# Attention and SwiGLU on one core: two queues for the first load of k, longer first dummies, and one bias moved

## The chip, the cores and the metric

The kernel runs on one core of a Trainium2 chip. A core has five engines with instruction streams of their own: TensorE (PE: matmuls and transposes into PSUM; its weight loads, PEld, overlap them), VectorE (DVE), ScalarE (ACT), GpSimd (POOL) and SyncE (SP). SP, ACT and POOL also issue DMAs. The metric is the device time of one execution in microseconds. The kernel before takes 332.2 us, the median of 4 runs (332.03 to 332.84).

## What is computed

Causal attention with a sliding window of 64, over 8 batches, 8 heads, 576 positions and 64 per head, followed by a SwiGLU feed-forward block over the 4608 tokens:

```python
scores = scale * np.matmul(q, k.transpose(0, 1, 3, 2))
mask = (rel >= 0) & (rel < window)          # window = 64
scores = np.where(mask, scores, -1000000000.0)
attn = np.exp(scores - max) ; attn = attn / sum
x = (attn @ v), heads side by side          # 4608 x 512
g = x @ w_gate ; silu = g * (1.0 / (1.0 + np.exp(-g)))
out = (silu * (x @ w_val)) @ w_out          # 512 -> 1536 -> 512
```

All inputs and the output are float32; the kernel computes its matmuls in bfloat16.

## The kernel before

The 4608 tokens are cut into 36 chunks of 128 for attention and 9 chunks of 512 for the feed-forward block. For a chunk n of attention, q and k are loaded with positions on partitions, transposed by TensorE (later by DMA), and copied from PSUM to `qT` and `kT`; 24 small matmuls give the scores (`S`, line 421), ScalarE takes the exponential into `pt` (line 431), matmuls with v give the sums (`A`, two phases, line 471), VectorE divides (`norm`, lines 490 and 493) into `xb`, and TensorE transposes the result (`X`, line 568) to `xT`. The feed-forward step `F` (line 602) takes 128 of the 1536 columns: four gate matmuls, four value matmuls, a tanh on ScalarE (608), and, in step `U`, two operations on VectorE (611, 613) into `hT`. `O` multiplies by `w_out`.

The order at the start is written out by hand. `LOADS` is the order in which loads are issued; `STEPS` the order of everything else. Each token makes instructions and appends them to the queue of their engine, and each engine runs its own queue strictly in that order, waiting on semaphores for what others make. The tokens that matter here:

- `f:0` (line 285): the first 128 positions of k, in two halves of four heads, into the float32 tile `ff`; both DMAs are issued by SP (line 290). It is the first token of `LOADS`, so it stands before everything else on its queue.
- `init`: clears and constants on VectorE: the zeros `wz` for dummies, the identity, the mask, and the bias mask `nmask` (line 268), then clears in `kT` and `va` (270, 272); and one exponential of ScalarE (line 256) that brings its table load forward.
- `q:0`, `kq:n`, `v:n`, `w:a:b`: loads issued by POOL, which convert to bfloat16. Their order: q0, q1, k1, q2, k2, v1, v0, q3, k3, v2, v3, then weights 7 to 8, 1, 5, chunks 4 and 5, weights 3, 4, 6, and so on.
- `ca:0:0`, `cd:0:1`: the casts of `ff` to the bfloat16 tile `cc`, half of the head pairs on ScalarE, half on VectorE (lines 299, 301). Each waits for both halves of `f:0`.
- `T:0:1`, `T:0:0`: the transposes of `cc`, two each (line 309); `ea:0:1` and `ed:0:0` copy them into `kT`.
- `TQ:n`, `TK:n`: four transposes of q or k of chunk n (309); `qa`, `qd`, `ka`, `kd`: the copy to `qT` or `kT` on ACT or DVE. `xa`, `xd`: the same for `X`.
- `warm:45:64` (line 339): 45 dummy matmuls of zeros, 64 columns each (line 345); nobody reads their result.
- `W:1` (`fill`, line 350): one dummy matmul of zeros with 512 columns (line 357).
- `B:n` (`bias`, line 396): two matmuls of 512 columns that put the mask of chunk n into the two PSUM banks of its scores ahead of them (line 401). Chunks 0, 1 and 3 have such a bias; for the others `M:n` multiplies the exponentials by the mask on VectorE (line 437).
- `ld:n`: loads of a later chunk.

The queue of TensorE follows the tokens; a dependency is only what data and buffers ask for. `fill` takes the bank that has been free longest and doesn't reserve it.

Of the kernel before, what the change touches and what calls it, by code (L numbers as in the profile page):

```python
# [7 lines left out]
B, H, S, D = 8, 8, 576, 64  # L8
DM, DFF = H * D, 1536
T = B * S  # L10
# [139 lines left out]
class _Kernel:  # L150
# [13 lines left out]
    v:4 w:9:10 w:0:1 kq:6 v:7 kq:7 w:10:12  # L164
    """
    STEPS = """
    warm:45:64 B:0 B:1 ca:0:0 cd:0:1 T:0:1 T:0:0 ea:0:1 TQ:0 ld:8 wo:0:6 ed:0:0 qa:0 W:1 TQ:1 S:0 qd:1 TK:1
    ld:9 kd:1 W:1 TQ:2 S:1 qd:2 TK:2 kd:2 W:2 S:2 W:1 A0:0 A0:1 A1:0 A1:1 ld:10 N:0 TQ:3 B:3 qa:3 N:1 TK:3 X:0
    ka:3 xa:0 M:2 W:1 S:3 X:1 A0:2 xd:1 A1:2 ld:11 N:2 W:1 A0:3 A1:3 N:3 W:1 X:2 F:0:7:0:256 xd:2 U X:3
    F:0:8:0:384 xd:3 F:0:1 U U F:0:5 U TK:4 TQ:4 ld:12 ka:4 TQ:5 F:0:7:256:512 qd:4 TK:5 qa:5 F:0:8:384:512 U  # L170
    S:4 U F:0:3 kd:5 M:4 S:5 U F:0:4 M:5 U F:0:6 U F:0:2 U A0:4 A0:5 A1:4 ld:13 wo:6:12 A1:5 F:0:9 N:4 N:5 X:4
    F:0:0 U xa:4 X:5 U TK:6 xa:5 TQ:6 ld:14 F:1:0:0:128 ka:6 U F:1:1:0:256 qa:6 TQ:7 U F:1:2:0:256 qd:7 S:6
    TK:7 U F:1:3:0:256 kd:7 F:0:10 M:6 U U A0:6 S:7 A1:6 ld:15 TQ:8 TK:8 N:6 F:0:11 M:7 ka:8 qd:8 X:6 A0:7
    xa:6 S:8 U A1:7 ld:16 F:1:4:0:384 N:7 F:1:5:0:384 U X:7 U TQ:9 xa:7 F:1:6:0:384 M:8 qa:9 TK:9 U F:1:7 kd:9
    TD:10 U A0:8 S:9 A1:8 ld:17 F:1:8 N:8 M:9 X:8 TQ:11 xa:8 F:1:9 U qd:11 A0:9 TK:11 U A1:9 ka:11 F:1:10 N:9
    TK:12 U X:9 ka:12 TQ:12 F:1:11 xd:9 qd:12 TD:13 S:10 U S:12 F:1:0:128:512 M:10 F:1:1:256:512 M:12 A0:10 U
    S:11 A1:10 U F:1:2:256:512 F:1:3:256:512 N:10 F:1:4:384:512 U XD:10 F:1:5:384:512 O:0:0 U U U M:11 O:0:1
    A0:11 S:13 A1:11 O:0:2 N:11 M:13 X:11 O:0:3 xd:11 F:1:6:384:512 U TD:14 TD:15
    """

    def __init__(self, nc, q, k, v, wg, wv, wo, out):
# [103 lines left out]
    def first_load(self, n):  # L285
        (_, b, s, L), = self.segs(128 * n, 128)
        for u in range(2):
            d = self.ff[n][64 * u:64 * u + 64].rearrange("p h j d -> p h (j d)")
            a = self.k[b, 4 * u:4 * u + 4, s:s + L, :].rearrange("h (p j) d -> p h (j d)", j=2)
            self.g.op("sp", lambda e, d=d, a=a: e.dma_start(d, a), writes=[("ff", n, u)], dma=True)  # L290

    def cast(self, n, half, eng):
        hs = slice(2 * half, 2 * half + 2)
# [489 lines left out]
```

The softmax here doesn't subtract the row's maximum and nothing guards it: scores larger than these inputs give would overflow.

## Time and profile before

| | |
|---|---|
| median of the 4 runs | 332.2 us (332.03, 332.04, 332.35, 332.84) |
| profiled execution, its own time | 331.92 us |
| span of its instructions | 329.8 us |
| busy TensorE, VectorE, ScalarE, GpSimd | 324.6, 217.2, 136.0, 116.5 us |
| gate and value matmuls (L602) | 2 x 468, 112.5 us each |
| output matmuls (L635) | 420, 97.8 us |
| first load of k, from issue to landing | 2.7 us (first half), 3.6 us (second) |
| first gate matmuls (chunk 0, column block 7) | start at 17.76 us |

The times of a view are microseconds from the start of the span. A busy row cuts the span into 40 slices of 8.2 us, each digit the busy share in tenths. In the timeline a line gives start, length, engine, line of the kernel, operation, what is written and read, how often, and in brackets the idle time before it with what ended it. In the chain of waits, which is followed back from the last instruction, each piece has its start and length; adjacent pieces of one kind are merged. A matmul's record contains the time to drain, so the distance between two starts tells the speed, not the length of one.

The first rows of the two queues that the change touches, from the timeline:

```profile
0.74 1.41 SPq L290 DMA_DIRECT2D ff<-in_k_dram  x2
0.74 1.28 ACT L256 ACT_TABLE_LOAD   x1 [0.74 <-PEq L768]
...
2.04 0.20 ACT L256 ACTIVATE wup<-wup 128x1 f32<-128x1 f32 x1
...
5.17 0.42 ACT L299 ACTIVATE cc<-ff 128x256 bf16<-128x256 f32 x1 [2.93 <-DMA ff<-in_k_dram]
```

SP issues the two halves one after the other; ScalarE loads its table, makes the dummy exponential, and then has nothing to do until the halves have landed.

### The profile page before, as it was taken

Reading aid. Unit: us, or ns where it says so; the run is one execution under the profiler, and the core shown is the slowest. Engines: PE = TensorE matmul, PEld = TensorE weight load, DVE = VectorE, ACT = ScalarE, POOL = GpSimd, SP = SyncE. Lnnn points to the kernel's source line nnn. Section 1 sums busy time; section 2 is a strip of 40 time slices with the busy share of each in tenths; the row PEclk is TensorE's granted clock in tenths of the full one; section 3 lists DMA queues with packets and bytes.
Section 4 is the critical chain, followed back from the end, with each engine's and each line's share of the span. In section 5 each row is a group of like instructions: output and inputs, shape, how many; then the busy total and the mean of one; then the engine's idle time right before and its main releaser. Section 6 shows DMA issues by size and latency. Waiting matters only on the chain.

```text
span 329.8 us, 8380 instructions
## 1 busy us (share of the span) xinstructions
PE 324.6 (98%) x3543; PEld 166.6 (51%) x3543; DVE 217.2 (66%) x457; ACT 136.0 (41%) x247; POOL 116.5 (35%) x145
## 2 busy tenths in 40 slices
PE   7999999999999999999999999999999999999996
PEld 5565665564455454544445454545454544444444
DVE  5589999993467858485857676767676766555520
ACT  3735566453344344343425252525243432332222
POOL 8999999957017506060706060100000000000000
PEclk9999999999999999999999999999999999999999
DMA  9999999999999999999999999442424111100012
GB/s 107 165 168 172 158 182 155 160 141 179 193 172 148 171 160 104 153 89 169 90 169 81 175 71 188 67 111 44 118 35 128 34 64 34 64 34 32 32 63 99
DMA packets 169365, 38.56 MB, mean 117 GB/s; under 512 B 160368, under 2 KB 164848, under 8 KB 169328
## 3 DMA queue, kind: packets, MB, share of 16 engines
q0 software_dynamic: 123600, 18.75, 85.7%
q1 hardware_dynamic: 45584, 19.21, 28.8%
q8 instruction: 28, 0.46, 0.6%
q10 hardware_dynamic: 144, 0.07, 0.1%
q14 instruction: 9, 0.07, 0.1%
HBM read 37.75 MB, written 9.44 MB: 143 GB/s over the span
## 4 chain that ended last, share of the span: by engine, by line
PE 97%; DVE 2%; issue 0%
PE ps L602 57%; PE ps L635 28%; PE ps L421 3%; PE ps L534 2%; PE ps L309 2%; PE ps L471 2%; PE ps L665 1%; PE ps L568 1%; PE ps L401 1%; PE ps L357 1%; DVE xb L493 1%; DVE mask L267 0%; DVE hT L613 0%; DVE pt L437 0%; DVE rc L490 0%
## 5 line engine op out<-in xcount | busy, mean ns | idle before, releaser
L611 DVE SCALAR_TENSOR_TENSOR uu<-sig,ps 128x512 bf16<-128x512 bf16 (+3 forms) x117 | 75.3, 643 | 66.0 <-ACT sig L608 65.7
L602 PE MATMUL ps<-xT,Wg 128*128 128x512 bf16 (+3 forms) x468 | 112.5, 363 | 0.1
L602 PE MATMUL ps<-xT,Wv 128*128 128x512 bf16 (+3 forms) x468 | 112.5, 363 | 0.0
L608 ACT ACTIVATE sig<-ps 128x512 bf16<-128x512 f32 (+3 forms) x117 | 66.0, 565 | 88.9 <-PE ps L602 88.8
L635 PE MATMUL ps<-Wo,hT 128*128 128x512 bf16 x420 | 97.8, 379 | 0.0
L613 DVE SCALAR_TENSOR_TENSOR hT<-uu,ps 128x512 bf16<-128x512 bf16 (+3 forms) x117 | 75.5, 645 | 4.0
L371 POOL DMA_DIRECT2D va<-in_v_dram x40 | 40.3, 1041 | 88.3 <-PE ps L534 86.6
L602 PEld LDWEIGHTS ps<-xT,Wv 128*128 128x128 bf16 x468 | 45.0, 98 | 48.8 <-DVE hT L613 0.5
L602 PEld LDWEIGHTS ps<-xT,Wg 128*128 128x128 bf16 x468 | 43.9, 98 | 45.9 <-DVE hT L613 0.2
L635 PEld LDWEIGHTS ps<-Wo,hT 128*128 128x128 bf16 x420 | 39.9, 98 | 46.6
L431 ACT ACTIVATE pt<-ps 128x512 bf16<-128x512 f32 x72 | 37.8, 600 | 27.0 <-PE ps L421 26.9
L647 ACT ACTIVATE ost<-ps 128x512 f32<-128x512 f32 x35 | 20.9, 597 | 66.0 <-PE ps L635 65.9
L283 POOL DMA_DIRECT2D qn<-in_q_dram x40 | 41.3, 1052 | 2.8 <-issue 2.0
L283 POOL DMA_DIRECT2D kn<-in_k_dram x39 | 40.6, 1062 | 1.0 <-DMA kn<-in_k_dram 1.0
L437 DVE TENSOR_TENSOR pt<-pt,mask 128x512 bf16<-128x512 bf16 x66 | 24.3, 418 | 0.2
L556 DVE TENSOR_TENSOR xb<-ps,rp 128x448 bf16<-128x448 f32 (+1 forms) x36 | 18.5, 514 | 1.2
L553 DVE RECIPROCAL rp<-ps 128x7 f32<-128x7 f32 (+1 forms) x36 | 6.7, 187 | 15.4 <-PE ps L534 15.4
L421 PE MATMUL ps<-qT,kT 64*64 64x64 bf16 (+1 forms) x864 | 16.0, 205 | 0.1
L421 PEld LDWEIGHTS ps<-qT,kT 64*64 64x64 bf16 x864 | 12.4, 109 | 7.0 <-DVE hT L613 4.2
L534 PE MATMUL ps<-va,pt 64*64 64x65 bf16 x728 | 11.5, 193 | 0.1
L493 DVE TENSOR_TENSOR xb<-ps,rc 128x256 bf16<-128x256 f32 x24 | 10.2, 424 | 0.8
L534 PEld LDWEIGHTS ps<-va,pt 64*64 64x64 bf16 x728 | 9.3, 108 | 0.6 <-DVE hT L613 0.4
(50 smaller groups left out, 106.3 us busy)
## 6 DMA issues: line engine op xcount, KB each, us to landing
out_dram<-ost SPq DMA_DIRECT2D x35, 256.0 KB, 2.8
qn<-in_q_dram POOLq DMA_DIRECT2D x32, 128.0 KB, 6.5
va<-in_v_dram POOLq DMA_DIRECT2D x32, 128.0 KB, 6.4
kn<-in_k_dram POOLq DMA_DIRECT2D x31, 128.0 KB, 7.5
Wo<-in_moe_w_out_dram POOLq DMA_DIRECT2D x2, 768.0 KB, 12.0
Wg<-in_moe_w_gate_dram POOLq DMA_DIRECT2D x8, 128.0 KB, 5.1
Wv<-in_moe_w_val_dram POOLq DMA_DIRECT2D x8, 128.0 KB, 5.1
Wg<-in_moe_w_gate_dram POOLq DMA_DIRECT2D x2, 256.0 KB, 5.4
```

The source lines that it names most:

```text
L283: self.g.op("pool", lambda e, d=d, a=a: e.dma_start(d, a), writes=ks, dma=True)
L371: g.op("pool", lambda e, d=d, a=a: e.dma_start(d, a), writes=ks, dma=True)
L421: r = e.matmul(sv[h][o:o + 64, c, q0:q1], self.kT[ps, c, kk:kk + 64], qT[ps, c, q0:q1], start=not biased, stop=not biased or c == 3 and kk ...
L431: g.op("act", lambda e, po=po, si=si: e.activation(po, si, ACTF.Exp, scale=SCALE), reads=[bk], writes=[pk])
L437: "dve", lambda e: e.tensor_tensor(po, po, m, ALU.mult), reads=[pk, "mask"], writes=[pk]))
L534: r = e.matmul(bb[b][0][ws, 65 * sl:65 * sl + 65], self.pt[(n + j) % self.NP][ks, h, ws], vv[ks, h, 0:65], start=m == q[0], stop=m == q[-1])
L602: r = e.matmul(bank[:, 0:n], W[:, kk, f * 128:f * 128 + 128], xT[:, kk, t0:t1], start=(kk == 0), stop=(kk == NK - 1))
L608: g.op("act", lambda e: e.activation(sig[:, 0:n], G[:, 0:n], ACTF.Tanh, scale=0.5), reads=[gk], writes=[("sig", i)])
L611: g.op("dve", lambda e: e.scalar_tensor_tensor(uu[:, 0:n], sig[:, 0:n], 1.0, G[:, 0:n], ALU.add, ALU.mult), reads=[("sig", i), gk], writes ...
L613: g.op("dve", lambda e: e.scalar_tensor_tensor(hT[:, f, t0:t1], uu[:, 0:n], 0.5, V[:, 0:n], ALU.mult, ALU.mult), reads=[("uu", i), vk], wr ...
L635: r = e.matmul(OB[:, :], hT[:, f, 128 * u:128 * u + 128], self.Wo[:, f, :], start=(f == 0), stop=(f == NF - 1))
L647: g.op("act", lambda e: e.activation(ost[:, :], OB[:, :], ACTF.Copy), reads=[ok], writes=[("ost", io)])
```

## The change

The second half of `f:0` is issued by ScalarE and not by SP. The 45 first dummies get 96 columns in place of 64. `B:1` goes from behind `B:0` to behind `TQ:0`. Of the eight dummies of 512 columns four go: one of the pair before `S:2`, the one behind `S:2`, the one behind `N:2` and the one before `X:2`; and the one behind `qa:0` goes to before `TQ:0`. The order of the loads stays; of the rest of `STEPS` only the line breaks differ.

```diff
-    warm:45:64 B:0 B:1 ca:0:0 cd:0:1 T:0:1 T:0:0 ea:0:1 TQ:0 ld:8 wo:0:6 ed:0:0 qa:0 W:1 TQ:1 S:0 qd:1 TK:1
-    ld:9 kd:1 W:1 TQ:2 S:1 qd:2 TK:2 kd:2 W:2 S:2 W:1 A0:0 A0:1 A1:0 A1:1 ld:10 N:0 TQ:3 B:3 qa:3 N:1 TK:3 X:0
-    ka:3 xa:0 M:2 W:1 S:3 X:1 A0:2 xd:1 A1:2 ld:11 N:2 W:1 A0:3 A1:3 N:3 W:1 X:2 F:0:7:0:256 xd:2 U X:3
...
+    warm:45:96 B:0 ca:0:0 cd:0:1 T:0:1 T:0:0 ea:0:1 W:1 TQ:0 B:1 ld:8 wo:0:6 ed:0:0 qa:0 TQ:1 S:0 qd:1 TK:1
+    ld:9 kd:1 W:1 TQ:2 S:1 qd:2 TK:2 kd:2 W:1 S:2 A0:0 A0:1 A1:0 A1:1 ld:10 N:0 TQ:3 B:3 qa:3 N:1 TK:3 X:0
+    ka:3 xa:0 M:2 W:1 S:3 X:1 A0:2 xd:1 A1:2 ld:11 N:2 A0:3 A1:3 N:3 X:2 F:0:7:0:256 xd:2 U X:3 F:0:8:0:384
...
-            self.g.op("sp", lambda e, d=d, a=a: e.dma_start(d, a), writes=[("ff", n, u)], dma=True)
+            self.g.op(("sp", "act")[u], lambda e, d=d, a=a: e.dma_start(d, a), writes=[("ff", n, u)], dma=True)
```

More of the change, by code (lines that the diff above doesn't have):

```diff
@@ L166 @@
     STEPS = """
-    warm:45:64 B:0 B:1 ca:0:0 cd:0:1 T:0:1 T:0:0 ea:0:1 TQ:0 ld:8 wo:0:6 ed:0:0 qa:0 W:1 TQ:1 S:0 qd:1 TK:1
-    ld:9 kd:1 W:1 TQ:2 S:1 qd:2 TK:2 kd:2 W:2 S:2 W:1 A0:0 A0:1 A1:0 A1:1 ld:10 N:0 TQ:3 B:3 qa:3 N:1 TK:3 X:0
-    ka:3 xa:0 M:2 W:1 S:3 X:1 A0:2 xd:1 A1:2 ld:11 N:2 W:1 A0:3 A1:3 N:3 W:1 X:2 F:0:7:0:256 xd:2 U X:3
-    F:0:8:0:384 xd:3 F:0:1 U U F:0:5 U TK:4 TQ:4 ld:12 ka:4 TQ:5 F:0:7:256:512 qd:4 TK:5 qa:5 F:0:8:384:512 U
-    S:4 U F:0:3 kd:5 M:4 S:5 U F:0:4 M:5 U F:0:6 U F:0:2 U A0:4 A0:5 A1:4 ld:13 wo:6:12 A1:5 F:0:9 N:4 N:5 X:4
@@ L172 @@
[L172 to L176, printed above, removed]
@@ L177 @@
-    S:11 A1:10 U F:1:2:256:512 F:1:3:256:512 N:10 F:1:4:384:512 U XD:10 F:1:5:384:512 O:0:0 U U U M:11 O:0:1
-    A0:11 S:13 A1:11 O:0:2 N:11 M:13 X:11 O:0:3 xd:11 F:1:6:384:512 U TD:14 TD:15
+    warm:45:96 B:0 ca:0:0 cd:0:1 T:0:1 T:0:0 ea:0:1 W:1 TQ:0 B:1 ld:8 wo:0:6 ed:0:0 qa:0 TQ:1 S:0 qd:1 TK:1
+    ld:9 kd:1 W:1 TQ:2 S:1 qd:2 TK:2 kd:2 W:1 S:2 A0:0 A0:1 A1:0 A1:1 ld:10 N:0 TQ:3 B:3 qa:3 N:1 TK:3 X:0
+    ka:3 xa:0 M:2 W:1 S:3 X:1 A0:2 xd:1 A1:2 ld:11 N:2 A0:3 A1:3 N:3 X:2 F:0:7:0:256 xd:2 U X:3 F:0:8:0:384
@@ new lines @@
+    xd:3 F:0:1 U U F:0:5 U TK:4 TQ:4 ld:12 ka:4 TQ:5 F:0:7:256:512 qd:4 TK:5 qa:5 F:0:8:384:512 U S:4 U F:0:3
+    kd:5 M:4 S:5 U F:0:4 M:5 U F:0:6 U F:0:2 U A0:4 A0:5 A1:4 ld:13 wo:6:12 A1:5 F:0:9 N:4 N:5 X:4 F:0:0 U
+    xa:4 X:5 U TK:6 xa:5 TQ:6 ld:14 F:1:0:0:128 ka:6 U F:1:1:0:256 qa:6 TQ:7 U F:1:2:0:256 qd:7 S:6 TK:7 U
+    F:1:3:0:256 kd:7 F:0:10 M:6 U U A0:6 S:7 A1:6 ld:15 TQ:8 TK:8 N:6 F:0:11 M:7 ka:8 qd:8 X:6 A0:7 xa:6 S:8 U
+    A1:7 ld:16 F:1:4:0:384 N:7 F:1:5:0:384 U X:7 U TQ:9 xa:7 F:1:6:0:384 M:8 qa:9 TK:9 U F:1:7 kd:9 TD:10 U
@@ L179 @@
+    A0:8 S:9 A1:8 ld:17 F:1:8 N:8 M:9 X:8 TQ:11 xa:8 F:1:9 U qd:11 A0:9 TK:11 U A1:9 ka:11 F:1:10 N:9 TK:12 U
+    X:9 ka:12 TQ:12 F:1:11 xd:9 qd:12 TD:13 S:10 U S:12 F:1:0:128:512 M:10 F:1:1:256:512 M:12 A0:10 U S:11
+    A1:10 U F:1:2:256:512 F:1:3:256:512 N:10 F:1:4:384:512 U XD:10 F:1:5:384:512 O:0:0 U U U M:11 O:0:1 A0:11
+    S:13 A1:11 O:0:2 N:11 M:13 X:11 O:0:3 xd:11 F:1:6:384:512 U TD:14 TD:15
     """
```

## The prediction

> **What bounds the kernel now.** I read the busy slices first, then the shares of the chain that ended last, then the first 20 us of that chain in order of time, and last the times from issue to landing of the early loads.
>
> ```profile
> PE   7999999999999999999999999999999999999996
> ...
> POOL 8999999957017506060706060100000000000000
> ...
> PE 97%; DVE 2%; issue 0%
> ```
>
> TensorE is busy throughout (its row is below 9 only in the first and the last slice of 8.2 us) and holds 97% of the chain, while POOL issues loads without rest for the first 70 us. So a microsecond is won or lost in the start, where TensorE still waits for others, and it stays won only if no later load is waited for. Here is the start in the chain's order (start, length, what):
>
> ```profile
> 4.33 1.89 PE ps L401 x4
> 6.21 0.85 PE ps L309 x8
> 7.07 0.43 PE ps L357
> ...
> 10.58 0.44 DVE kT L301
> ...
> 11.50 0.32 PE ps L357
> 11.83 0.65 PE ps L471 x38
> 12.72 0.42 DVE xb L493
> ...
> 14.79 0.68 DVE pt L437 x2
> ...
> 16.23 0.32 PE ps L357
> ...
> 17.20 0.32 PE ps L357
> 17.53 0.40 PE ps L568 x4
> 17.92 0.87 PE ps L602 x8
> ...
> 19.02 4.86 PE ps L602 x24
> ```
>
> Biases, transposes and scores run to 11.8, attention and VectorE's normalizing to 18.9, and from 19.0 gate and value matmuls stand back to back. Dummies (L357) are links of this chain at 7.07, 11.50, 16.23 and 17.20. Rows of the timeline show the speed, and the cast that waits for the first load of k:
>
> ```profile
> 1.02 2.58 PE L345 MATMUL ps<-wz 128*128 128x64 bf16 x45 [1.02 <-DVE wz L255]
> ...
> 4.33 1.89 PE L401 MATMUL ps<-nmask,ident 128*128 128x512 bf16 x4 [0.72 <-DVE nmask L268]
> ...
> 5.17 0.72 DVE L301 CAST cc<-ff 128x256 bf16<-128x256 f32 x1 [0.59 <-DMA ff<-in_k_dram]
> ...
> 12.79 0.59 PE L401 MATMUL ps<-nmask,ident 128*128 128x512 bf16 x2
> ```
>
> The same bias matmul comes every 0.42 us at 4.33 ((1.89-0.63)/3) and every 0.21 at 12.79: the clock doubles between. The transposes at 9.25 are the first with a faster member, so it doubles at about 9.6; the windows' clock column reads 1.00 all along and does not show it. TensorE stood still for 0.72 us before 4.33, and ran with hardly a gap from 4.33 to the doubling, 5.3 us. Two single loads, seen by their tiles, matter below, chunk 0 of v and chunk 3 of k:
>
> ```profile
> L371 POOL DMA_DIRECT2D va<-in_v_dram x1: 923/923/923, 6.6 to 6.6; - x1
> ...
> DMA to landing us min/median/max: 4.2/4.2/4.2
> ```
> ```profile
> L283 POOL DMA_DIRECT2D kn<-in_k_dram x1: 942/942/942, 8.3 to 8.3; - x1
> ...
> DMA to landing us min/median/max: 4.7/4.7/4.7
> ```
>
> They land at 6.65+4.2 = 10.85 and 8.32+4.7 = 13.02. POOL issues without a pause, so these are dates that no faster TensorE can move.
>
> **The dummies, 45 of 96 columns.** 64 columns come every 53 ns (first to last start, 2.35 us over 44), so 96 take 80 ns: the block ends at 1.02+45*0.080 = 4.62, not 3.5. The bias mask is ready at 4.27, so the bias starts 0.29 later than before. In exchange the 0.72 us of standing still is gone.
>
> **Bias of chunk 1 moved, a dummy put before TQ:0.** Bias 0 alone takes 4.62 to 5.47 (2 x 0.42). Bias 1 (0.85 slow, 0.43 fast) goes behind TQ:0, where TensorE would wait for the copy of q0 anyway (S:0's wait at 7.85 was for that copy); the one dummy (0.43) now fills behind the first transposes, not between TQ:0 and TQ:1.
>
> **The second half of k on ScalarE's queue.** It was issued at 1.48 behind its sister and landed 3.6 us later, at 5.1; the first took 2.7 us, to 3.44. Issued at 0.74 it lands between 0.74+2.7 = 3.4 and 0.74+3.6 = 4.3. ScalarE's issue (0.60 to 0.75, SP's rows) pushes its table load (1.28) and dummy exponential (0.20) to about 3.0; its next work is the cast, which waited 2.93 us for this load, so that costs nothing. Without that cover it would cost the 0.75. VectorE clears tiles until 4.58, so the cast runs 4.58 to 5.30, and the first transpose (needs 5.36) follows the bias at 5.47, without a gap. Before, it began at 6.01.
>
> The Trainium skill speaks against this edit (DMA: Bandwidth & Descriptors, "Issuing engines are not separate DMA queues"): transfers of several issuers share the same 16 DMA engines, so a second issuer saves only the time of issuing. By that rule the half lands at about 5.1-0.74 = 4.4, still under 4.58, so the sum is the same either way.
>
> **The clock.** TensorE is now unbroken from 1.02. The trace doesn't show what the clock would do then; the nearest row is the 5.3 us from the last stop to the doubling, which gives 1.02+5.3 = 6.3. The lower end is 3.6, since the 2.58 us of dummies by themselves did not bring it; the upper end is no change, 9.6. I take 6.3, by the row that is unbroken work as this is.
>
> The skill's rule (TensorE: Matmul & The Clock Gate, Part 1) is that the clock rises after one busy window of about 3.4 us whose phase the kernel does not choose; the trace's 5.3 us lies inside the 3.4 to 6.8 that this allows. By the rule the clock would come somewhere from 4.4 to 7.8.
>
> **The sum to attention.** At slow speed T:0:1 and T:0:0 take 5.47 to 5.90, the dummy to 6.33; from there fast: TQ:0 to 6.55, bias 1 to 6.98, TQ:1 to 7.2. The copy of q0 (0.60) starts at 6.75, S:0 at 7.45 (before 7.85). TK:1 7.8, its copy 8.2 to 8.63, S:1 8.7 (before 9.77). TK:2 waits for k2, landing at 4.87+4.2 = 9.07; copy to 9.95; S:2 10.0 to 10.35 (before 11.06). A0:0 now waits for v0 and starts at 10.9, before 11.76: **0.85 us earlier**, with half a microsecond of slack: an earlier clock gains nothing more, and a clock as late as 7.8 only uses the slack up (S:2 by 10.9).
>
> **The sum to the feed-forward.** Normalizing 0 and 1 is VectorE's 2.28 us, so 0.85 carries on: 13.9, masks of chunk 2 to 14.6. Chunk 3 does not follow: TK:3 waits for k3 until 13.08 (before 13.22), so its copy, S:3 and both exponentials are 0.14 earlier, done at 15.72. A0:2 runs 14.7 to 15.4 and N:2 starts 0.8 earlier; A0:3 waits for those exponentials, 15.82 instead of 16.48 (the dummy that stood at 16.15 is out, 0.32). Its end, 16.54, releases N:3, which with xd:2 takes 1.5 us: xd:2 ends at 18.1 (before 18.89), and F:8 starts at 18.2 instead of 18.95. **-0.75 us.** F:7's value weights land at 11.66+5.7 = 17.36, just when they are asked for.
>
> Removed dummies, eight down to four: those at 16.15 and 17.12 and one of the pair at 10.38 stood inside waits for VectorE, worth nothing beyond what is counted; the one at 11.44 (0.32) stood before A0:0 and is worth 0.3 if the clock does not come earlier.
>
> **Does it stay?** Behind 19 us TensorE asks 0.75 earlier for loads that come no earlier. Tightest: q5 lands 18.02+5.3 = 23.3, asked for at 24.17-0.75 = 23.4; k6 at 32.57+5.1 = 37.7, asked for at 38.54-0.75 = 37.8; k5 and q7 have 0.2 to 0.35. All hold, barely; a miss costs 0.1. The extra ScalarE semaphore at the end waits for a load long landed.
>
> The profiled run took 331.92 around a span of 329.8 and lies 0.28 under the median of 332.2. Its own time less 0.75 is 331.2, the median less 0.75 is 331.45; a clock that comes at different moments in different runs would explain such a spread, and the change takes most of that away, so I take 331.35.
>
> **Rivals.**
> 1. *The clock comes no earlier* (9.6). For it: dummies multiply zeros, and the 0.72 us may not be what held it back. Then S:0 comes at 8.03, S:2 again at 11.06, and only the missing dummies before A0:0 and A0:3 count, one after the other on the same path as far as chunk 3 allows: 0.3. 331.9.
> 2. *The clock is lost or late between 10 and 18 us (slower).* TensorE has fewer dummies there and the busy row of its windows was already 0.85, 0.90, 0.66, 0.92 from 13 to 17; now the waits for v0, q3 and the exponentials (0.5+0.7+0.4) are open. If they halve the clock at about 15, and it comes back 5.3 us later as at the start, the 3.4 us from F:7 at 16.9 to 20.3 run at half speed and lose 1.7: +1.7-0.75 = +0.95, 333.15. It decides once the clock is still missing at F:7 (17 us). Against it: before, 0.66 in a microsecond cost no clock.
> 3. *ScalarE's load is late, so the edit does not do what it says.* If the table load goes first (1.28), the issue is at 2.02 and landing at 4.7 to 5.6; the cast ends up to 6.35, TensorE stands 0.9 us behind the bias and the clock is back at 9.6 or later, now with bias 1 and a dummy in front of S:0: about +0.5, 332.7. Against it: in program order the load comes first.
> 4. *Loads land earlier too*, since the half of k no longer runs beside them at 3.7 to 4.7: up to 0.35 more, 331.0. Against it: v0's 4.2 us is the same as its neighbours'.
>
> **Numbers.** Forecast 0.58, rivals 0.20, 0.09, 0.07, 0.06. The forecast's own range is 331.1 to 331.65 (gain 0.55 to 1.1). 0.2% is 0.66 us, about what a measurement of this kernel can tell from no change; the line lies at 331.54, so of the forecast 0.47 is faster and 0.11 the same. With rival 4 and a little of rival 1 faster is 0.56; same 0.30 (rival 1 most of it, half of rival 3); slower 0.14 (rival 2, the rest of 3). The range 330.8 to 332.6 leaves out rival 2, the worst of rival 3 and the best of rival 4.
>
> **What would show it.** Right: no gap before the first bias; 128-column transposes at half duration by about 6.3 to 7.8; A0:0 at 10.9; F:8 near 18.2 and the rest shifted whole. Wrong: bias 0 to first transpose with a gap (rival 3), TQ:2 still slow (rival 1), gate matmuls of 512 columns at 0.43 spacing behind 17 us (rival 2), or a TensorE wait on a load behind 19 us, which would give the gain back.

## The result and the profile after

The changed kernel takes **332.74 us** (median of 34 runs, 331.31 to 334.15), the kernel before 332.14 (53 runs, 331.51 to 333.30). The ratio is 1.0017, 95% interval 1.0010 to 1.0023: it became slower by some 0.6 us, where 0.8 us less was forecast. The profiled execution took 332.44 us, its span 330.3 (before 331.92 and 329.8).

Everything up to 10 us went as meant, and even earlier. The page first, then rows of the timeline (start, length):

```profile
PE   7789999999999999999999999999999999999996
...
POOL 8999999966007606060706060100000000000000
...
PE 94%; DMA 2%; POOL 2%; DVE 2%; issue 0%; ACT 0%; POOLq 0%
```
```profile
0.74 0.71 ACTq L290 DMA_DIRECT2D ff<-in_k_dram  x1
...
1.02 3.30 PE L345 MATMUL ps<-wz 128*128 128x96 bf16 x45 [1.02 <-DVE wz L255]
...
4.15 0.42 ACT L299 ACTIVATE cc<-ff 128x256 bf16<-128x256 f32 x1 [1.16 <-DMA ff<-in_k_dram]
...
4.33 0.60 PE L401 MATMUL ps<-nmask,ident 128*128 128x512 bf16 x2
...
4.50 0.51 DVE L301 CAST cc<-ff 128x256 bf16<-128x256 f32 x1
...
5.07 0.40 PE L309 MATMUL ps<-ident,cc 128*128 128x128 bf16 x4
...
12.03 0.91 PE L471 MATMUL ps<-va,pt 64*64 64x65 bf16 x56 [1.59 <-DMA va<-in_v_dram]
...
19.22 0.82 PE L602 MATMUL ps<-xT,Wg 128*128 128x384 bf16 x4
```

The rows of the kernel before for the first attention matmuls, the transposes of chunk 3 of k, and the gate matmuls of column block 8 (F:8 from here on):

```profile
11.76 0.86 PE L471 MATMUL ps<-va,pt 64*64 64x65 bf16 x56
...
13.22 0.39 PE L309 MATMUL ps<-ident,kn 128*128 128x128 bf16 x4
...
18.95 0.82 PE L602 MATMUL ps<-xT,Wg 128*128 128x384 bf16 x4
```

No gap stands before the bias, the two biases are 0.2 us apart, so the clock is already doubled at 4.33, and the first transposes come at 5.07 (before 6.01). But TensorE's row falls to 8 in the second slice, the chain of waits has 2% DMA and 2% POOL in it that were not there, and the first attention matmuls start at 12.03, later than before (11.76). The chain in order of time says why:

```profile
6.60 5.38 DMA va<-in_v_dram
...
12.03 0.72 PE ps L471 x40
...
12.99 0.42 DVE xb L493
...
15.05 0.68 DVE pt L437 x2
...
17.79 0.40 PE ps L568 x4
18.19 0.87 PE ps L602 x8
```

The load of chunk 0 of v, issued at 6.6 as before, landed 5.4 us later, not 4.2. From there each step comes 0.27 us later than before: F:8 at 19.22 (18.95). At 24.7 the transposes of chunk 5 of q wait once more, 0.28 us: that load, issued at 18.03, landed after 6.6 us (before 5.3), at 24.59. (The view names a step of VectorE that ended at 24.65; in the kernel before the same transposes started while that step still ran, so it is the load.) Together that makes 0.55. At 46 us TensorE makes good 0.23 of it, where the kernel before waits, and by 157 us it has lost 0.21 again; the span grew by 0.5.

### The profile page after: what moved, and what is told of

It reads as the page before. It is cut to its first block, busy times and chain, and to the rows that moved or that the text cites. A ratio compares the mean times of both kernels' runs of the same rounds, so it can differ in the third digit from the quotient of the medians.

```text
span 330.3 us, 8373 instructions
## 1 busy us (share of the span) xinstructions
PE 322.6 (98%) x3539; PEld 165.7 (50%) x3539; DVE 216.8 (66%) x457; ACT 136.0 (41%) x247; POOL 116.5 (35%) x145
## 4 chain that ended last, share of the span: by engine, by line
PE 94%; DMA 2%; POOL 2%; DVE 2%; issue 0%; ACT 0%; POOLq 0%
PE ps L602 57%; PE ps L635 28%; PE ps L421 3%; PE ps L534 2%; DMA va<-in_v_dram 2%; PE ps L471 1%; PE ps L309 1%; POOL qn L283 1%; PE ps L665 1%; DVE xb L493 1%; PE ps L568 1%; POOL kn L283 1%; POOL va L371 0%; DVE rc L490 0%; DVE uu L611 0%
## 5 line engine op out<-in xcount | busy, mean ns | idle before, releaser
L371 POOL DMA_DIRECT2D va<-in_v_dram x40 | 39.5, 1020 | 89.5 <-PE ps L534 87.7
L283 POOL DMA_DIRECT2D qn<-in_q_dram x40 | 40.5, 1031 | 2.9 <-issue 2.1
L283 POOL DMA_DIRECT2D kn<-in_k_dram x39 | 39.8, 1041 | 0.3 <-DMA kn<-in_k_dram 0.3
L493 DVE TENSOR_TENSOR xb<-ps,rc 128x256 bf16<-128x256 f32 x24 | 10.2, 424 | 0.8
```

The source lines that it names most:

```text
L283: self.g.op("pool", lambda e, d=d, a=a: e.dma_start(d, a), writes=ks, dma=True)
L371: g.op("pool", lambda e, d=d, a=a: e.dma_start(d, a), writes=ks, dma=True)
```

## The experiments

Each kernel was timed in five rounds beside the kernel before. A run's mean granted clock is given too: a stretch of 3.4 us at half speed in a span of 330 makes it 1 - 3.4*0.5/330 = 0.995.

### The parts one at a time

**Both halves of k on SyncE again**, everything else as changed:

```diff
-            self.g.op(("sp", "act")[u], ...
+            self.g.op("sp", ...
```

> The changed kernel with both halves of k on SyncE again. Theory A (the loads are late because the instruction fetch of 16 KB falls on one DMA engine while v0 is in it): the fetch still comes near 9.9 us, v0 lands late again, 11.7 to 12.0, first attention matmuls at 11.8 to 12.0, time 332.4 to 332.8. Theory B (the two-queue load of k leaves some DMA engines behind): v0 lands at 10.8 to 11.0, attention starts at about 11, time 331.4 to 331.7.

332.16 us (11 runs), ratio 1.0009 (0.9997 to 1.0022); 4 of the 11 runs had a mean clock near 0.995, of which more below. The cast starts at 6.01, the first transposes at 6.82, 1.75 us later than in the changed kernel, and still attention starts at 11.67 and F:8 at 18.89, both earlier than there. The fetch of instructions came at 10.92, not at 9.9 as theory A had it. v0 landed at 11.62, because one of the 16 parts of each load was 0.75 us behind from the first load on, so theory B's 10.8 to 11.0 failed as well. In these two profiles the second queue won 1.75 us for the first transposes, and none of it reached F:8.

**The queue alone**, in the kernel before:

```diff
-            self.g.op("sp", ...
+            self.g.op(("sp", "act")[u], ...
```

> The kernel before with only the second half of k moved to ScalarE's queue. Theory A (instruction fetch): TensorE's order is that of before, so the loads land as before within 0.2 us and the time is that of before or up to 0.2 us less. Theory B (two-queue load): v0, q3 and k3 land 0.6 to 1.2 us later than before, time 0.3 to 0.8 us more.

332.33 us (12 runs), 1.0009 (0.9997 to 1.0021). **The width of the first dummies alone:**

```diff
-    warm:45:64 B:0 B:1 ...
+    warm:45:96 B:0 B:1 ...
```

> The kernel before with only the first dummies made 96 columns wide. Both theories: SyncE's load of k is as before, so the first transposes start near 6.0. If unbroken work brings the clock early, the rows up to 9.6 us run at double speed; the gain is bounded by loads to 0.3 us. If Theory A (instruction fetch) holds and the fetch comes before 9.95 us, v0 lands late and the time is 0.2 to 0.6 us more than before; otherwise same as before within 0.2 us.

332.49 us (11 runs), 1.0004 (0.9994 to 1.0013). In both profiles the clock came early (transposes of q2 at 8.6, before at 9.25), attention started at 11.13 and 11.27, 0.5 to 0.6 sooner than before, and then the transposes of k3 stood at 13.73 and 13.82 (before 13.22): k3 landed at 13.6 and 13.7. F:8 came no earlier (19.43 and 19.04). Neither part alone makes the loss, no run of either had a mean clock under 0.999, and an earlier clock alone makes no gain. With the queue alone TensorE's start is that of the kernel before, gap and all, and yet the clock doubled at 7.0 and not at 9.6: the moment differs from run to run.

### Why the loads are late

**Fewer instructions in front.** The queue named instruction brings packets of 16 KB (28 in the run, 0.46 MB) that took 0.9 to 2.1 us each in the changed kernel. Its first, in the DMA view of 9.85 to 9.95 us (packets, MB, and the time that the packets took as a share of 16 engines in that window; it can exceed 100%, since a packet counts whole where it starts):

```profile
q0 software_dynamic: 95, 0.01, 189.9%
q8 instruction: 1, 0.02, 60.9%
```

That is 0.609*16*0.1 = 0.97 us of one engine. It starts there while v0 is in flight. 17 dummies of 256 columns take the slow clock as long as 45 of 96 and make 56 instructions fewer:

```diff
-    warm:45:96 B:0 ...
+    warm:17:256 B:0 ...
```

> The changed kernel with 17 first dummies of 256 columns in place of 45 of 96: the same TensorE time at slow clock (3.63 against 3.60 us), 28 matmuls and 28 weight loads fewer in TensorE's instruction stream. Theory A (instruction fetch): the first fetch moves later, to 11 us or more, v0 lands at 10.8 to 11.0, time 331.4 to 331.7. Theory B (two-queue load): the fetch may move, but v0 still lands at 11.5 or later, time 332.4 to 332.8.

The packet moved to 12.0 us. Rows of this kernel's timeline:

```profile
11.25 0.87 PE L471 MATMUL ps<-va,pt 64*64 64x65 bf16 x56 [0.66 <-DMA va<-in_v_dram]
12.09 0.40 PE L309 MATMUL ps<-ident,qn 128*128 128x128 bf16 x4
...
14.26 0.38 PE L309 MATMUL ps<-ident,kn 128*128 128x128 bf16 x4 [1.34 <-DMA kn<-in_k_dram]
```

v0 now landed at 11.2 and not at 12.0, and the delay had gone to k3: 14.1 after 13.4. The time rose to 333.47 us (9 runs), 1.0052 (1.0025 to 1.0079): theory A was right that v0 would be sooner and wrong about the time. The late k3 is only part of the rise: in the profile F:8 comes at 19.48, 0.53 later than before, and 0.77 more is lost in one wait at 50.2 us whose cause the profile does not show. 4 of the 9 runs lost the clock (see below), but the 5 others, too, have a median of 333.22; why is open.

In the trace's completions it is mostly the last of a load's 16 parts that is held up: for v0 of the changed kernel 11.98, against 11.30 and 10.91 for the two parts ahead of it. The loads behind keep some of the delay (q3 landed 0.3 and k3 0.4 later than before). Among the profiles with all loads, the packet came before 9.9 us in three (the changed kernel, its repeat, and the one with its dummies back), and there v0 landed at 11.6 to 12.0. With a packet from 10.0 to 10.7 (before and three others) v0 got through by 10.8 to 11.2 and q3 and k3 were hit. In two profiles with a packet at 10.9 v0 was late as well: with both halves on SyncE for the reason given there, and in one below (four dummies in the gap), where 15 parts of v0 were in by 11.16 and the last came at 13.02.

**Are the loads the wall?** One load was left out: chunk 1 of q, so that everything behind it is issued 0.87 us sooner. The first try kept the order of the rest:

```diff
-    f:0 init q:0 kq:1 kq:2 ...
+    f:0 init q:0 k:1 kq:2 ...
-        iq = n % self.NQ
+        iq = n % self.NQ if (which, n) != ("q", 1) else 0
```

> The changed kernel with the four dummies back and without the load of chunk 1 of q (chunk 0 of q is used for it, so its output is not the reference's): every load from chunk 1 of k on is issued one place, 0.87 us, earlier. If the loads are the wall of the changed kernel's start (v0 for the first attention matmuls, k3 for the transposes of chunk 3), attention starts 0.4 to 0.9 earlier, F:8 at 18.1 to 18.5, median 331.2 to 331.6. If TensorE or VectorE is the wall, F:8 and the time stay within 0.2 us of the kernel with the load (e6).

It took 368.37 us, since `ld:8`, which refills the buffer of chunk 0 of q, stood before the transpose that now reads it: TensorE waited 36.5 us for chunk 8. It says nothing on the question. With `ld:8 wo:0:6` put behind `TQ:1`, for the kernel before and for the changed one with its dummies back:

> The kernel before without the load of chunk 1 of q (chunk 0 of q is used for it, so the output is not the reference's; the load of chunk 8 goes behind that transpose in the order): every load from k1 on is issued 0.87 us earlier. If TensorE at its slow clock, not the loads, sets the start of the kernel before, attention starts within 0.3 us of 11.76 and the median falls by 0.0 to 0.3 us (331.8 to 332.2). If the loads set it there too, the median falls by 0.5 to 0.9 (331.2 to 331.6).

> The changed kernel with the four dummies back and without the load of chunk 1 of q, with the load of chunk 8 behind that transpose (the earlier try made the transpose wait for chunk 8). If the loads are the wall of the changed kernel's start, attention starts at 10.7 to 11.2, F:8 at 18.0 to 18.4, median 331.2 to 331.7, 0.5 to 0.9 below the same kernel with the load (332.35). If not, within 0.2 us of it.

The kernel before fell to 331.67 us (9 runs), ratio 0.9970 (0.9959 to 0.9981); the other to 331.06 (12 runs), 0.9962 (0.9949 to 0.9975), beside 332.35 and 1.0001 with the load. (The profile of the latter is of the one run of 12 that lost the clock, 332.80, so its F:8, at 20.29, says nothing on the forecast 18.0 to 18.4; its attention started at 10.71.) So both are bound by the loads in the start, **the kernel before too**. Its timeline without q1:

```profile
11.05 0.86 PE L471 MATMUL ps<-va,pt 64*64 64x65 bf16 x56
11.84 0.40 PE L309 MATMUL ps<-ident,qn 128*128 128x128 bf16 x4
12.60 0.38 PE L309 MATMUL ps<-ident,kn 128*128 128x128 bf16 x4
...
18.25 0.82 PE L602 MATMUL ps<-xT,Wg 128*128 128x384 bf16 x4
```

Transposes of k3 0.62 earlier, F:8 0.70 earlier. The clock came early in this profile too (by 7.3 us), but it did so in the two with all loads above, where F:8 stayed at 19.0 to 19.4.

### Where the rest went: the clock

23 of the changed kernel's 34 runs had a mean clock of 0.994 or 0.995 (the expectation below counts 24), two more had 0.99; of the 93 runs of the kernel before beside the experiments none was under 0.999.

> The changed kernel unaltered, for a second profile and more runs. 24 of its 34 runs showed a mean granted clock of 0.994 or 0.995, no run of the kernel before did (0.999 to 1.0). Theory C (the clock is lost once in the start because four dummies are out): again more than half of the runs at 0.994 to 0.995, and those slower by 0.3 to 1 us than the others; a profile of such a run shows like matmuls at half speed for some 3 us between 12 and 25 us. Theory A (instruction fetch and late loads alone): the clock column is accidental, and runs at 0.995 and at 1.0 take the same time.

332.96 us (12 runs), 1.0017 (0.9998 to 1.0035); 8 of 12 runs below 0.998, with a median of 333.09, the 4 others 331.77. The profile this time was of such a run. Its stretches of 2 us (sum of times, busy TensorE, weight loads, VectorE, ScalarE, POOL, granted clock, DMA share, GB/s):

```profile
8.00:10.00 2.00, 1.63 (x57) 1.09 (x57) 0.96 (x3) 1.54 (x3) 2.00 (x3) 1.00 2.22 148
10.00:12.00 2.00, 0.19 (x18) 0.08 (x6) 0.00 (x0) 1.08 (x2) 2.00 (x4) 1.00 2.37 148
12.00:14.00 2.00, 1.97 (x62) 1.63 (x63) 0.95 (x4) 0.26 (x1) 2.00 (x4) 0.52 2.06 136
14.00:16.00 2.00, 2.00 (x35) 1.30 (x33) 1.86 (x7) 1.32 (x3) 2.00 (x3) 0.62 1.47 191
16.00:18.00 2.00, 1.64 (x80) 1.06 (x70) 1.20 (x5) 1.19 (x3) 2.00 (x4) 1.00 1.70 188
```

TensorE is done with its scores at 10.2, stands until v0 lands, and then the clock is halved: 2*(1-0.52)/0.5 + 2*(1-0.62)/0.5 = 3.4 us. F:8 comes at 19.82, 0.87 later than before. The stretch from 10 to 12 in the other profile of the changed kernel, which kept its clock, and in the kernel before:

```profile
10.00:12.00 2.00, 0.44 (x24) 0.33 (x24) 0.00 (x0) 1.22 (x3) 2.00 (x4) 1.00 2.29 144
```
```profile
10.00:12.00 2.00, 1.91 (x79) 1.11 (x69) 0.72 (x2) 1.54 (x3) 2.00 (x4) 1.00 2.44 158
```

In these rows the TensorE that starts at slow clock is busy all the way to attention; the one with the early clock is done 1.6 us before the load that it needs, with its dummies gone.

The trace's record of the clock gives the moments. In the three profiles that lost it in the start (leaving aside the first try without q1: this one, the one without q1 above, and the one with four dummies in the gap below) it doubled at 5.26, 6.39 and 5.20 and was halved at 12.09, 13.21 and 18.85: two, two and four times 3.41 us later, and each time for 3.41 us. In the stretch of 3.41 us just before the halving TensorE was busy 1.20, 1.68 and 2.16 us. In the profile of the changed kernel that kept its clock the doubling was at 3.65; counted from there, the wait for v0 falls into the stretch from 10.48 to 13.89, of which TensorE was busy 1.86 us. So how the wait falls into these stretches, and with it the moment of the doubling, seems to decide as well as its length. A bound for the busy time does not come out of this: 2.16 us lost the clock, 1.86 kept it, and 1.82 in a stretch of the kernel with 17 dummies kept it too.

**The four dummies back**, in the changed kernel:

```diff
-    ... kd:2 W:1 S:2 A0:0 ...       N:2 A0:3 A1:3 N:3 X:2 ...
+    ... kd:2 W:2 S:2 W:1 A0:0 ...   N:2 W:1 A0:3 A1:3 N:3 W:1 X:2 ...
```

> The changed kernel with the four dummies back that it left out (second before S:2, behind S:2, behind N:2, before X:2). Theory C (clock lost): all runs at a clock of 0.999 to 1.0, median 331.9 to 332.3, 0.4 to 0.8 below the changed kernel. Theory A (late loads alone): clock as it may be, median 332.6 to 332.9, since the loads are as late.

332.35 us (12 runs), 1.0001 (0.9985 to 1.0018); one run of 12 lost the clock. **The same four out of the kernel before** (the diff the other way round):

> The kernel before without the same four dummies. Theory C (clock lost): at least some runs at 0.994 to 0.995, since TensorE is as idle from 11 to 18 us; median 332.3 to 332.9. Theory A (late loads alone): no lost clock, TensorE starts attention 0.2 to 0.3 earlier, median 331.8 to 332.2.

332.22 us (12 runs), 0.9997 (0.9979 to 1.0016), below what theory C had put; two of 12 lost the clock, at 333.13 and 333.22. Leaving out the dummies is thus not enough to make the loss: in this profile attention starts at 11.03 without a gap behind the scores. That the smaller gap is why the same dummies matter less there is not tested by itself. **Four dummies only in the gap before attention:**

```diff
-    ... S:2 A0:0 A0:1 ...
+    ... S:2 W:4 A0:0 A0:1 ...
```

> The changed kernel with four dummies of 512 columns (0.86 us at full clock) behind S:2, where TensorE stands for 1.6 to 1.8 us until v0 has landed; the other removed dummies stay out. Theory C (the clock is lost because of this gap): all runs but one or two at 0.999 to 1.0, median 331.7 to 332.2. If the clock is lost because of the dummies taken out behind it (N:2, X:2), more than half of the runs still show 0.994 to 0.995 and the median stays at 332.6 to 332.9.

332.43 us (12 runs), 0.9997 (0.9985 to 1.0010), above the median that theory C had put; two of 12 lost the clock. So the gap before attention is where the changed kernel mostly loses it: 33 of its 46 runs without dummies behind S:2, 2 of 12 with them. (With the early start and no dummies behind S:2 it was also lost in 4 of 11 runs with both halves on SyncE and 4 of 9 with 17 dummies; with dummies there, in 1 of 12 in each of three kernels.) It isn't the only place: the profile of this kernel is one of the two, and there v0 came at 13.0 and the clock fell behind a later thin stretch, as two windows show:

```profile
16.00:19.00 3.00, 1.74 (x76) 1.18 (x71) 2.40 (x10) 1.18 (x3) 3.00 (x6) 0.98 1.70 182
19.00:22.00 3.00, 3.00 (x18) 2.19 (x17) 2.33 (x7) 0.38 (x1) 3.00 (x6) 0.50 2.25 158
```

**v0 ahead of v1**, with the dummies in the gap:

```diff
-    ... kq:2 v:1 v:0 kq:3 ...       S:2 A0:0 A0:1 A1:0 A1:1
+    ... kq:2 v:0 v:1 kq:3 ...       S:2 W:4 A0:0 A1:0 A0:1 A1:1
```

> As the kernel with four dummies in the gap, and v0 loaded ahead of v1, with the second phase of chunk 0 ahead of the first of chunk 1. If the late v0 is what holds the changed kernel's start, attention begins at 10.2 to 11.1, normalizing of chunk 0 some 1 us earlier, F:8 at 18.3 to 18.7, median 331.4 to 331.8. If k3 and the exponentials of chunk 3 hold it, F:8 and the median are those of the kernel with four dummies in the gap, within 0.2 us.

332.47 us (12 runs), 1.0000 (0.9986 to 1.0014). v0 was there at 10.15, but v1 landed at 12.6 and k3 at 13.9; F:8 at 19.28. No order of these two helps while k3 is late. None of the versions with all loads beats the kernel before beyond its interval.

## Why the prediction was wrong

- **Dummies, bias, second queue, clock: right.** 45 dummies without a gap; the second half of k landed at 3.53 (3.4 to 4.3 was said), though the first, still on SP, came at 4.06 and not at 3.44, and the cast needs both; the first transposes at 5.07 (5.47); the clock at 3.65 (between 3.6 and 9.6, 6.3 taken; in the repeat 5.26). S:2 started at 9.99, where 10.0 was said. Part of the gain over 11.76 was an accident of the profile that it was read from: with TensorE's start as before the clock doubled at 9.65 there, at 8.4 in the kernel without the four dummies and at 7.0 with the queue alone, where attention started at 11.13.
- **"These are dates that no faster TensorE can move": the first step that failed.** It is true that TensorE cannot make them earlier. It can make them later: packets of instructions come over the same DMA engines, and the one at 9.88 us met v0. v0 was put at 10.85 (in the profile before it landed at 10.80) and landed at 11.98, k3 was put at 13.02 and landed at 13.39. Of the 0.85 us to attention -0.27 was left. That the packet follows TensorE's instruction stream rests on one profile each (17 dummies moved it by 2.2 us, and the delay from v0 to k3); why the held-up part lags 0.6 us in one profile and 1.9 in another is open.
- **The wall was misread for the kernel before as well.** The sum took its start to be TensorE's time at slow clock, with rows such as the dummy at 11.50 as links of the path. Without q1 that kernel gains as much as the profile's F:8 said, 0.70, and 0.84 in the medians (331.67 against 332.51 beside it). There, too, k3 stands behind what the chain shows as TensorE: TK:3 began 0.2 us after the load had landed. Slack of 0.1 to 0.3 us, read from one execution, was treated as a plan; the landings of k3 spread over 13.0 to 14.1 us in the profiles with all loads.
- **"Does it stay? All hold, barely": failed.** q5 was to land at 23.3 and landed at 24.59; TensorE waited 0.28. The value weights of F:7, put at 17.36, "just when they are asked for", landed at 18.00, and at 18.71 with the queue alone, where TensorE waited 0.39 us for them.
- **Removed dummies "worth nothing beyond what is counted": the step that decided the sign.** In the changed kernel they mostly kept the clock in the waits: without them 33 of 46 runs lost it (median 332.87) and 13 did not (331.92), with them 1 of 12. The prediction put what they do for the clock at nothing. Rival 2 had the mechanism and 0.09 of the chance. That its price, 333.15, came out near is in good part luck: it lost 1.7 us at F:7, from 16.9 on, less a gain of 0.75; measured were about 0.9, with the halving from 12.1 to 15.5 in the one profile of the changed kernel that shows it, and hardly any gain. The argument against it was that a microsecond at 0.66 had cost nothing before; the waits that it named itself come to 1.6 us.

The Trainium skill (TensorE: Matmul & The Clock Gate, "Why this matters for your kernels") advises against idle gaps over some 3 us between bursts of matmuls, since one window of idleness halves the clock. Here a gap of 1.84 us before attention was enough in the profile that shows the loss, so for this kernel that advice is too loose. The length of the halved stretch, 3.41 us, agrees with the window of about 3.4 us in Part 1 of that page. The range of 4.4 to 7.8 that the prediction worked out from that window holds five of seven profiles of the changed kernel and its variants; 3.65 and 4.05 lie below it. The other estimate from the skill (DMA: Bandwidth & Descriptors, "Issuing engines are not separate DMA queues"), 4.4 for the second half of k, was later than the measured 3.53, and than the 4.06 at which both halves had landed.

Taken together: the earlier clock gained nothing by itself, and the late loads took most or all of the forecast gain. The runs that kept the clock have medians of 332.26 and 331.77 in the two series, beside 332.14 and 332.11 for the kernel before; the profiled one, 332.44, is among the slower of them. Losing the clock, in three runs of four, costs about 0.9 (332.87 less 331.92, a split of runs and not an experiment; that the loss goes when the dummies come back is one). The changed kernel's median is made by the runs that lost it.

## What to carry to other kernels

Before speeding up an engine in a start, leave out one load and see whether the time moves: if it does, as here by 0.84 us, the loads are the wall whatever the chain of waits names, and a faster engine only waits longer. Dummies that seem to stand idle inside a wait may be what holds the clock; count how long the engine will stand without them after the speed-up, not before it. And look at the mean clock of every run, since one profile may be of the quarter that shows nothing.

## What was not expected of the hardware

- Instructions come in 16 KB packets, 28 in the run, the first of them 0.97 us of one DMA engine's time in the changed kernel. In the start, the last part of the load in flight then landed 0.6 to 1.9 us behind the last but one (q3 of the kernel before, v0 with four dummies in the gap), and the loads behind it were late as well.
- With unbroken dummies from 1.02 us the clock doubled at 3.7, 4.1, 5.2, 5.2, 5.3, 5.5 and 6.4 us in seven profiles of the changed kernel and its variants: a spread of 2.7 us from run to run.
- The half clock lasted 3.41 us in each of the three profiles, with TensorE busy throughout. Where TensorE waited 36.5 us, in the first try without q1, it lasted 37.55.
